# A written-out list of steps, one PSUM pool, and unsplit band scores in every batch

## The chip, the core and the metric

The kernel runs on one core of one Trainium2 chip. The metric is the device time of one execution in microseconds (us). A profile shows the core's engines: PE is TensorE (PEld its weight loads), DVE is VectorE, ACT is ScalarE, POOL is GpSimd, SP issues the transfers.

## What is computed

Two layers follow each other, for 4 batches of 768 positions. Layer one is attention with 8 heads of 64 channels in which position i sees the 128 positions up to itself and the first 4 (the sinks). Its output x (768 x 512) goes into layer two: four experts, each a causal attention over all 768 positions with one head of 64 channels, weighted by a gate that keeps the best 2 of 4 experts.

```
scores = q @ k.T / 8 ;  keep = (key < 4) | (0 <= row - key < 128)        # layer one
x = softmax(where(keep, scores, -1e9)) @ v                               # per head, then heads side by side
logits = x @ w_gate ; w = softmax over the two largest                   # layer two
out = sum over the two experts e of  w_e * (causal_softmax((x wq_e)(x wk_e).T / 8) @ (x wv_e) @ wo_e)
```

Everything is float32. A matmul of the kernel either takes float32 operands as they are ("exact" in the code), or each operand is split into a rounded part and its remainder, both float32r, and three products are added up (`THREE`).

## The kernel before

The work is cut into units. A unit of kind 0 ("first") is a pair of heads of one batch in layer one: 16 of them. A unit of kind 1 ("second") is a pair of experts of one batch in layer two: 8 of them. Two heads (or experts) always go together: one lies on partitions 0 to 63, the other on 64 to 127.

A first unit loads q, k and v (`first`), turns q and k so that channels lie on partitions (`Pair.turn_by_pe` in batch 0 on PE, `Pair.turn` in the others on DVE, L799 and L803), computes scores row by row (128 positions each): `band_scores`, on PE, 260 columns (two key blocks and the sinks) or 128 in the first row. In batches 0 and 1 (`EXACT`) the scores are float32 matmuls of `qn` with `kx` (L820). In batches 2 and 3 ACT writes the rounded part (L804), POOL the remainder (L808), into the tiles `qs` and `ks`, and PE does three float32r matmuls per head (L825). Then DVE picks and takes the row minimum (L1078, L1081; L1047 in the first two rows), ACT takes exp (L1085, L1052), DVE sums (L866, L867), POOL scales (L1059, L1104), PE transposes the probabilities (L878), ACT or DVE copies them out of PSUM (L707, L709) or DVE multiplies them by a triangle (L922), and PE multiplies them with v into an accumulator `Acc` (L851, L855). The sum leaves PSUM as a rounded part and a remainder of x (L690 on ACT, L695 on DVE).

A second unit projects x (L1177, 48 matmuls for q and as many for k), splits the result into `qs` and `ks` (L757 on ACT, L760 on DVE), and does wide causal rows the same way (L825, L981, L989, L996, L878, L851). Per batch there are also the values and the gate (L1204) and the output projection (L1251).

PE's array is used in four ways: transposes ("ROWS" in the code) and scores ("rows") address it as two halves of 64 rows, 64*128 in a profile; L851 addresses it as two halves of 64 columns, 128*64 ("cols"); projections use all of it, 128*128 ("FULL"). L525 (`fill`) is a matmul of zeros that the planner puts where it sees PE idle within the first 130 us, L1262 ten such at the start.

What stands when on an engine is decided before the program is built. Every piece of work is a `Step` with a priority, a cost, the steps it comes after and the buffers that it makes and uses; `Plan.emit` simulates the five engines and always takes the step that can begin earliest, for PE by priority with a charge for changing the way the array is used. `NUDGE` adds to the priorities, by kind, unit and number. Buffers are rings, `kinds`: 6 PSUM banks for all but the accumulators (`b`), 2 for the accumulators (`acc`), 2 of each of `qs` and `ks`, 9 of `p` (probabilities), 3 of `pt` (transposed ones). A step can't be placed until its ring has a free slot.

Of the kernel before, what the change touches and what calls it, by code (L numbers as in the profile page):

```python
# [34 lines left out]
PSUM = ("b", "acc")  # L35

NUDGE = {
    "busy_PE": 5.2, " ": -68.2, " busy_PE": 82.2, " busy_PE 0": 78.2, "sink_values_DVE": 13.5, " sink_values_DVE": -16.5,
    "load_SP": -45.6, " load_SP": 39.9, "again_SP": 20.9, " again_SP": 56.7, "sink_values_ACT": -27.6,
    " sink_values_ACT": 7.3, "sink_values_POOL": 52.1, " sink_values_POOL": 35.8, "sink_values_SP": -45.0,  # L40
    " sink_values_SP": -24.6, "weight_ACT": -52.5, " weight_ACT": 53.4, "weight_POOL": -34.8, " weight_POOL": 46.3,
    "000 ": -73.5, "000 load_SP": -144.1, "tr_PE": -1.9, "000 tr_PE": -132.5, "000 tr_PE 0": -105.3, "fn_DVEACT": -11.6,
    "000 fn_DVEACT": 132.8, "000 tr_PE 1": -54.6, "go_POOL": 0.7, "000 go_POOL": -36.7, "000 tr_PE 2": -47.6,
    "000 tr_PE 3": -19.2, "spread_POOL": -14.3, "000 spread_POOL": -25.7, "differences_POOL": 6.4,
    "000 differences_POOL": 24.4, "band_scores_PE": 0.5, "000 band_scores_PE": -115.3, "000 band_scores_PE 0": 8.1,
    "low_DVE": -53.0, "000 low_DVE": -79.5, "exp_ACT": 45.8, "000 exp_ACT": 63.9, "go_DVE": -42.9, "000 go_DVE": -204.0,
    "norm_POOL": -27.0, "000 norm_POOL": -84.7, "000 tr_PE 4": 23.5, "av_PE": -0.2, "000 av_PE": -0.9, "000 av_PE 0": -50.3,
    "000 band_scores_PE 1": -19.2, "000 tr_PE 5": -41.0, "000 av_PE 1": -26.4, "000 band_scores_PE 2": -53.5,
    "pick_DVE": -45.8, "000 pick_DVE": -22.7, "000 band_scores_PE 3": -19.7, "keep_POOL": -10.3, "000 keep_POOL": 6.5,
    "000 tr_PE 6": 35.3, "tri_DVE": -62.4, "000 tri_DVE": 59.9, "of_sinks_PE": -0.3, "000 of_sinks_PE": -1.5,  # L50
# [241 lines left out]
}  # L292

HURRY = 30.10
STAY = 41.79
BULK = -8.35
FILL_COST, FILL_KEEP, FILL_END = 220.0, 0.0, 130000.0
# [26 lines left out]
class Step:  # L324


    def __init__(self, prio, cost, fn, after, new, use, moves, mode, behind):
# [15 lines left out]
        for b in (*new, *use):  # L343
            b.users.append(self)


class Plan:
# [31 lines left out]
    def emit(self):  # L379
# [19 lines left out]
        for s in self.steps:  # L399
            if not s.waiting:  # L400
                put(s)
# [955 lines left out]
```

## Time and profile before

| | |
|---|---|
| median of 3 runs | 393.12 us (392.98 to 393.4) |
| span of the profiled execution, first to last instruction | 391.6 us |
| the execution's own time | only its span is recorded; the runs' median is 1.5 us above it |
| PE, DVE, ACT, POOL busy | 383.9, 309.4, 271.7, 261.1 us |
| matmul records on PE | 4508 |

Busy time is the union of an engine's records. Matmuls are pipelined and the ends of their records are modelled, so one that waits for its turn inside the array still counts as busy; what a group of matmuls costs is better read from the starts of the records. A float32 matmul has two records, a float32r one has one.

### The profile page before, as it was taken

The numbers are of one execution on the slowest core, as the hardware profiler recorded it, in microseconds if no ns is written. First come the engines' busy times: TensorE is split into PE (matmuls) and PEld (weight loads), VectorE is DVE, ScalarE is ACT, GpSimd is POOL, SyncE is SP. The second block draws the span as 40 slices with busy tenths as digits, with TensorE's granted clock in tenths as the row PEclk, the third lists the DMA queues.
The fourth block names the chain that finished last, engine by engine and source line by source line (L and its number), as shares of the span: only waits on it lengthen the run. The fifth ranks groups of instructions, "written<-read, shape, count | busy, mean of one in ns | idle before, by whom it ended". The sixth has DMA issues, their size and how long they took to land.

```text
span 391.6 us, 12873 instructions
## 1 busy us (share of the span) xinstructions
PE 383.9 (98%) x4508; PEld 325.8 (83%) x4508; DVE 309.4 (79%) x1424; ACT 271.7 (69%) x971; POOL 261.1 (67%) x461
## 2 busy tenths in 40 slices
PE   8999999999999999999999999999999999999995
PEld 7767878988888888988888888988888888987874
DVE  6899998787999969679889959688689806648943
ACT  3898986266999957468869958459678804717830
POOL 5669999236999983568959854479958730038840
PEclk9999999999999999999999999999999999999999
DMA  7989997321165251523506100223000000012003
GB/s 164 224 159 169 186 181 131 56 42 44 42 109 97 44 107 56 83 83 83 82 3 121 44 0 5 40 110 95 2 3 2 3 3 2 2 54 110 3 28 134
DMA packets 124032, 28.42 MB, mean 73 GB/s; under 512 B 120576, under 2 KB 120576, under 8 KB 123968
## 3 DMA queue, kind: packets, MB, share of 16 engines
q1 hardware_dynamic: 123968, 27.61, 33.7%
q8 instruction: 35, 0.57, 0.6%
q14 instruction: 29, 0.24, 0.2%
HBM read 21.05 MB, written 6.29 MB: 70 GB/s over the span
## 4 chain that ended last, share of the span: by engine, by line
PE 83%; DVE 8%; POOL 3%; issue 2%; ACT 2%; DMA 1%; POOLq 0%; ACTq 0%; SPq 0%; DVEq 0%
PE acc L851 18%; PE b L1177 18%; PE b L825 13%; PE b L878 11%; PE b L1204 9%; PE b L1251 9%; PE b L820 4%; DVE b L1078 1%; DVE p L1081 1%; PE b L1262 1%; PE acc L855 1%; POOL p L1059 1%; DVE p L981 1%; DMA vn<-in_v_dram 1%; POOL v L680 1%
## 5 line engine op out<-in xcount | busy, mean ns | idle before, releaser
L996 POOL TENSOR_TENSOR p<-p,st 128x128 f32<-128x128 f32 (+5 forms) x96 | 87.3, 935 | 1.3
L707 ACT ACTIVATE pt<-b 128x256 f32<-128x256 f32 (+3 forms) x175 | 63.4, 397 | 12.5 <-PE b L878 8.8
L989 ACT ACTIVATE p<-p,st 128x384 f32<-128x384 f32 (+5 forms) x96 | 63.6, 669 | 9.4 <-DVE st L981 9.0
L825 PE MATMUL b<-ks,qs 64*128 64x260 f32 (+4 forms) x672 | 69.4, 323 | 0.3 <-DVE pt L922 0.2
L825 PEld LDWEIGHTS b<-ks,qs 64*128 64x128 f32 x672 | 52.9, 186 | 4.7 <-ACT pt L707 0.9
L878 PE MATMUL b<-ident,p 64*128 64x64 f32 x1120 | 55.1, 228 | 0.2 <-POOL p L1059 0.2
L878 PEld LDWEIGHTS b<-ident,p 64*128 64x128 f32 x1120 | 44.3, 138 | 11.7 <-issue 6.4
L1085 ACT ACTIVATE p<-p,st 128x132 f32<-128x132 f32 x128 | 51.1, 407 | 3.8 <-DVE st L1081 3.6
L981 DVE CUSTOM_DVE_ANT_0 p<-b,cmask 128x384 f32<-128x384 f32 (+3 forms) x96 | 45.3, 506 | 1.4 <-PE b L825 1.1
L851 PE MATMUL acc<-pt,v 128*64 128x128 f32 x672 | 45.5, 278 | 0.6 <-DVE pt L709 0.5
L851 PEld LDWEIGHTS acc<-pt,v 128*64 128x64 f32 x672 | 36.2, 136 | 7.1 <-issue 3.9
L851 PE MATMUL acc<-pt,vn 128*64 128x128 f32 x448 | 41.5, 283 | 0.3 <-ACT p L989 0.3
L709 DVE COPY pt<-b 128x256 f32<-128x256 f32 (+3 forms) x81 | 34.6, 446 | 8.3 <-PE b L878 7.9
L1204 PE MATMUL b<-wvh,x 128*128 128x260 f32 x192 | 35.8, 285 | 0.0
L1059 POOL TENSOR_TENSOR p<-p,st 128x520 f32<-128x520 f32 (+1 forms) x32 | 26.5, 835 | 13.5 <-DVE st L867 9.8
L1177 PE MATMUL b<-x,wqh 128*128 128x256 f32 (+1 forms) x128 | 33.2, 344 | 0.1
L1104 POOL TENSOR_TENSOR p<-p,st 128x512 f32<-128x512 f32 x32 | 33.2, 1041 | 0.0
L1177 PE MATMUL b<-x,wkh 128*128 128x512 f32 (+1 forms) x128 | 32.8, 341 | 0.0
L1251 PE MATMUL b<-woh,y 128*128 128x512 f32 x96 | 32.7, 402 | 0.0
L1081 DVE CUSTOM_DVE_ANT_0 p<-b,pair_mask 128x132 f32<-128x132 f32 x128 | 32.6, 288 | 0.0
L1078 DVE COPY_PREDICATED b<-earlier,b 128x128 f32<-128x128 int32 x128 | 31.2, 287 | 0.5 <-PE b L820 0.3
L1052 ACT ACTIVATE p<-p,st 128x260 f32<-128x260 f32 (+1 forms) x64 | 29.0, 459 | 3.7 <-DVE st L1047 2.9
(132 smaller groups left out, 919.0 us busy)
## 6 DMA issues: line engine op xcount, KB each, us to landing
vn<-in_v_dram SPq DMA_DIRECT2D x32, 192.0 KB, 3.2
out_dram<-o SPq DMA_DIRECT2D x24, 256.0 KB, 2.0
qn<-in_q_dram SPq DMA_DIRECT2D x52, 96.0 KB, 2.4
kn<-in_k_dram SPq DMA_DIRECT2D x52, 96.0 KB, 2.4
qn<-in_q_dram SPq DMA_DIRECT2D x6, 192.0 KB, 4.2
kn<-in_k_dram SPq DMA_DIRECT2D x6, 192.0 KB, 4.3
o<-in_moe_wo_dram SPq DMA_DIRECT2D x2, 256.0 KB, 3.7
v<-in_moe_wk_dram SPq DMA_DIRECT2D x4, 128.0 KB, 3.5
```

The source lines that it names most:

```text
L707: nc.scalar.activation(dst(), src(), AF.Copy)
L825: nc.tensor.matmul(o, self.qs.t[hs, a, qs], self.ks.t[hs, b, ks], start=n == 0, stop=n == 2)
L851: nc.tensor.matmul(o[e * 64:e * 64 + 64], lhs, rhs, start=e not in self.begun, stop=last and self.done == len(self.steps))
L878: nc.tensor.transpose(t[g].t[:, n, :], x[gs], ident[gs, gs])
L981: nc.vector.tensor_tensor_reduce(out=one(e)[:, cs], in0=s2[e].t[:, :(c1 - c0) * 128], in1=mask(c0, c1), scale=times, scalar=st.t[:, 3, es] ...
L989: nc.scalar.activation(x, x, AF.Exp, bias=st.t[:, 0, es], scale=-1.0, accum_out=st.t[:, 1, es])
L996: nc.gpsimd.tensor_mul(x, x, st.t[:, 2, e:e + 1].to_broadcast([128, n * 128]))
L1081: nc.vector.tensor_tensor_reduce(out=p.t[:, n, :], in0=s2[e].t[:, :SW], in1=pair_mask, scale=-scale, scalar=BIG, op0=OP.add, op1=OP.min, a ...
L1085: nc.scalar.activation(p.t[:, n, :], p.t[:, n, :], AF.Exp, bias=st.t[:, 0, n:n + 1], scale=-1.0, accum_out=st.t[:, 1, n:n + 1])
L1177: nc.tensor.matmul(t.t, w[a][:, c, es], X[b, c].t[:, x, cs], start=c == 0 and m == 0, stop=c == NCH - 1 and m == 2)
L1204: nc.tensor.matmul(t.t[:, :VW], X[b, c].t[:, a, qs], W["wv"][w][:, c, :], start=c == 0 and n == 0, stop=c == NCH - 1 and n == 2)
L1251: nc.tensor.matmul(t.t, Y[b, c].t[:, a, qs], W["wo"][w][:, c, :], start=c == 0 and n == 0, stop=c == EP - 1 and n == 2)
```

## The change

- `NUDGE`, `HURRY`, `STAY`, `BULK` and the search in `emit` go. A string `ORDER` lists all 2702 steps by number; a letter behind a number says which engine does a copy that ACT and DVE could both do (281 `a`, 119 `v`). `emit` goes through the list, gives each step its buffers, and issues it. What an engine does follows the list. `lined_up` stands for other shapes only.
- `fill_in` is the old fill rule, on the times that the list gives.
- `EXACT` is (0, 1, 2, 3): the split of q and k in layer one (ACT L804, POOL L808) and its three products per head are gone in batches 2 and 3; there too scores are float32 matmuls of `qn` with `kx`.
- `qs` and `ks` have one buffer each, used by second units only. `p` has 11, `pt` has 4. The accumulators share one pool of 8 PSUM banks with all else.

In both programs PE does the same transposes (1280), the same L851 (688), sinks (64) and projections (816). Float32 score matmuls go from 96 to 192, float32r ones from 672 to 384, fills from 44 to 10.

```diff
-PSUM = ("b", "acc")
-NUDGE = {
-    "busy_PE": 5.2, " ": -68.2, " busy_PE": 82.2, " busy_PE 0": 78.2, "sink_values_DVE": 13.5, " sink_values_DVE": -16.5,
...
-HURRY = 30.10
-STAY = 41.79
-BULK = -8.35
+PSUM = ("b",)
+ORDER = """
+0 46 1 52 44 49 53a 54v 51v 50a 64 65 39 55 40 75 78 41 47 45 76 59 60a 86 90 61a 67 56 58v 57v 93 79 143 87 91 77 80 81 142
...
     def emit(self):
-        for s in self.steps:
-            s.prio += sum(NUDGE.get(name, 0.0) for name in s.part)
...
+        listed = ORDER.split()
+        if len(listed) == len(self.steps):
+            order = []
+            for word in listed:
+                s = self.steps[int(word.rstrip("av"))]
+                order.append((s, {"a": ACT, "v": DVE}.get(word[-1]) or next(iter(s.cost))))
+        else:
+            order = self.lined_up()
+        free, moved, mode = dict(FREE), 0.0, "FULL"
+        for s, e in order:
+            t, taken = max([0.0] + [p.end + LATENCY[p.eng, e] for p in s.after] + [p.begun for p in s.behind]
+                           + [b.idle(e) for b in s.banks]), {}
+            for b in s.new:
+                at, n = self.slot(b.tag, e, taken.get(b.tag, ()))
+                taken.setdefault(b.tag, []).append(n)
+                b.slot, t = n, max(t, at)
...
             if e == PE and free[PE] < FILL_END:
...
+                self.fill_in(free[PE], t + turn, mode, s.mode)
...
+            s.fn()
...
-    kinds = {"qn": (3, 768, F32), "kn": (2, 768, F32), "vn": (3, 768, F32), "qs": (2, 2 * S, F32R), "ks": (2, 2 * NB * SW, F32R),
+    kinds = {"qn": (3, 768, F32), "kn": (2, 768, F32), "vn": (3, 768, F32), "qs": (1, 2 * S, F32R), "ks": (1, 2 * NB * SW, F32R),
-             ... "p": (9, 768, F32), "dv": (2, 512, F32), "pt": (3, 1024, F32), ...
+             ... "p": (11, 768, F32), "dv": (2, 512, F32), "pt": (4, 1024, F32), ...
-             "b": (6, 512, F32), "acc": (2, 512, F32)}
+             "b": (8, 512, F32)}
...
-            self.b = buf("acc", 512)
+            self.b = buf("b", 512)
...
-    EXACT = (0, 1)
+    EXACT = (0, 1, 2, 3)
```

What the list does to the order is seen on the engines. First PE, in the last batch's second units, behind their last scores. Before (L825 scores, L851 probabilities times values into an accumulator, L878 transposes):

```order
L825 MATMUL b_122<-ks_73,qs_72 128x384
L851 MATMUL acc_126<-pt_98,v_0_83 64x128 x6
L878 MATMUL b_124<-ident,p_87 128x64
L878 MATMUL b_123<-ident,p_87 128x64
...
L851 MATMUL acc_126<-pt_99,v_0_83 64x128 x6
L878 MATMUL b_121<-ident,p_88 128x64
L878 MATMUL b_120<-ident,p_88 128x64
...
```

and now, at the same place (L652, L678 and L705 are the same three; `b_127` is the accumulator):

```order
L652 MATMUL b_120<-ks_72,qs_71 128x384
L705 MATMUL b_121<-ident,p_93 128x64
L705 MATMUL b_125<-ident,p_93 128x64
...
L678 MATMUL b_127<-pt_98,v_0_81 64x128 x6
L678 MATMUL b_127<-pt_97,v_0_81 64x128 x6
L678 MATMUL b_127<-pt_100,v_0_81 64x128 x4
L705 MATMUL b_124<-ident,p_90 128x64
```

Before, four transposes stand between two pieces of column work and the array turns to columns for six matmuls at a time; now sixteen matmuls on three `pt` buffers follow each other. Over the program the column stretches (L851 and fills, 128*64) number 92 before and 56 now. Split at the first projection: 21 and 71 before, 12 and 44 now. The turns between FULL and the 64-row ways go from 29 to 41 behind the first projection. Between the last score of one second unit and the first of the next (seven such places) PE's row now has 104 to 254 other matmuls; the fewest, 104, are 36 of a projection with 512 columns, 44 transposes, 20 L851 and 4 band scores.

Second DVE, just ahead of the write of x that the first projection waits for (L695, the fourth tile x of batch 0). Before (L1078 pick, L1081 and L1047 row minimum, L799 turning of k):

```order
L799 STREAM_TRANSPOSE kx_82<-kn_67 128x3x128
L922 TENSOR_TENSOR pt_99<-b_120,own 128x4x64
L922 TENSOR_TENSOR pt_99<-b_124,own 128x4x64
L1081 ISA p_87,st_116<-b_123,pair_mask 128x132
...
L1047 ISA p_86,st_113<-b_121,bmask_138 128x128
L1047 ISA st_113 128x1
L695 SCALAR_TENSOR_TENSOR x_78<-acc_125,x_78 128x512
```

and now (L905, L908, L749, L626, L522 are the same statements):

```order
L749 TENSOR_TENSOR pt_98<-b_126,own 128x4x64
L905 COPY_PREDICATED b_124<-earlier,b_124 128x128
L908 ISA p_88,st_115<-b_124,pair_mask 128x132
L908 ISA st_115 128x1
L626 STREAM_TRANSPOSE kx_80<-kn_67 128x3x128
L522 SCALAR_TENSOR_TENSOR x_76<-b_121,x_76 128x512
L874 ISA p_94,st_117<-b_123,bmask_139 128x128
```

The row minimum of the next unit's first row (now L874) has moved behind the write. Counted from the program's start up to and with that write, DVE does 207 pieces of work before and 202 now: four copies of turned q or k fewer (they went to ACT), two copies of `pt` fewer and four of `sk` more, three first-row minima fewer, two turnings on DVE fewer, one pick and one minimum more.

## Rows read from the trace of the kernel before

**Rows 1.** The page, parts 1 and 2: busy time of PE and DVE, granted clock

```profile
PE 383.9 (98%) x4508; PEld 325.8 (83%) x4508; DVE 309.4 (79%) x1424; ACT 271.7 (69%) x971; POOL 261.1 (67%) x461
...
PEclk9999999999999999999999999999999999999999
```

**Rows 2.** Windows: us, busy PE, PEld, DVE, ACT, POOL, PEclk, DMA share, GB/s

```profile
10.00:20.00 10.00, 9.73 (x132) 7.25 (x129) 8.96 (x55) 8.76 (x41) 7.10 (x15) 1.00 1.02 224
...
120.00:140.00 20.00, 19.92 (x271) 17.36 (x269) 19.71 (x91) 19.59 (x70) 19.18 (x32) 1.00 0.35 67
```

**Rows 3.** Timeline at the first projection: start, us, engine, line, tiles, count

```profile
53.31 0.69 DVE L695 SCALAR_TENSOR_TENSOR x<-acc,x 128x512 fp32r<-128x512 f32 x1
...
53.93 0.74 PE L1177 MATMUL b<-x,wqh 128*128 128x512 f32 x2
```

**Rows 4.** Groups of DVE from 0 to 54 us: busy us, mean ns, idle before

```profile
L1081 DVE CUSTOM_DVE_ANT_0 p<-b,pair_mask 128x132 f32<-128x132 f32 x36 | 9.3, 285 | 0.0
L1078 DVE COPY_PREDICATED b<-earlier,b 128x128 f32<-128x128 int32 x37 | 9.2, 285 | 0.5 <-PE b L820 0.3
...
L1047 DVE CUSTOM_DVE_ANT_0 p<-b,bmask 128x128 f32<-128x128 f32 x11 | 2.8, 282 | 0.1
...
L709 DVE COPY kx<-b 128x192 f32<-128x192 f32 x7 | 2.3, 351 | 1.2 <-PE b L878 1.2
L799 DVE STREAM_TRANSPOSE qn<-qn 128x384 f32<-128x384 f32 x4 | 2.2, 560 | 0.0
```

**Rows 5.** Timeline of PE where the array turns, at 121 and at 234 us

```profile
121.38 0.41 PE L878 MATMUL b<-ident,p 64*128 64x64 f32 x8
121.61 1.27 PE L825 MATMUL b<-ks,qs 64*128 64x384 f32 x12
122.81 0.88 PE L851 MATMUL acc<-pt,vn 128*64 128x128 f32 x12
123.62 0.28 PE L878 MATMUL b<-ident,psk 64*128 64x64 f32 x2
123.73 0.41 PE L878 MATMUL b<-ident,p 64*128 64x64 f32 x8
124.07 0.44 PE L851 MATMUL acc<-pt,vn 128*64 128x128 f32 x4
...
234.32 1.77 PE L851 MATMUL acc<-pt,v 128*64 128x128 f32 x28
236.02 1.09 PE L878 MATMUL b<-ident,p 64*128 64x64 f32 x28
```

**Rows 6.** Timeline of PE: three band-score steps in a row, exact, then split

```profile
110.56 1.57 PE L820 MATMUL b<-kx,qn 64*128 64x260 f32 x12
112.06 0.88 PE L851 MATMUL acc<-pt,v 128*64 128x128 f32 x12
...
182.64 1.76 PE L825 MATMUL b<-ks,qs 64*128 64x260 f32 x18
184.34 0.88 PE L851 MATMUL acc<-pt,v 128*64 128x128 f32 x12
...
202.54 1.31 PE L825 MATMUL b<-ks,qs 64*128 64x260 f32 x18
203.78 0.66 PE L851 MATMUL acc<-pt,vn 128*64 128x128 f32 x8
```

**Rows 7.** Groups by line, whole span: the remainder of q, wide splits, fills

```profile
L808 POOL TENSOR_TENSOR qs<-qn,qs 128x384 fp32r<-128x384 f32 x16 | 16.3, 1017 | 3.4 <-ACT qs L804 3.2 <-DMA vn<-in_v_dram 0.2
...
L760 DVE TENSOR_TENSOR qs<-b,qs 128x512 fp32r<-128x512 f32 (+1 forms) x16 | 8.8, 553 | 15.3 <-ACT qs L757 15.3
...
L757 ACT ACTIVATE qs<-b 128x512 fp32r<-128x512 f32 (+1 forms) x16 | 7.9, 492 | 13.6 <-PE b L1177 13.4
...
L525 PE MATMUL b<-nought 128*64 128x128 f32 x60 | 4.5, 286 | 0.0
```

**Rows 8.** The chain that ended last, merged: start, us, engine, line, count

```profile
310.02 17.15 PE b L1177 x96
```

More of the change, by code (lines that the diff above doesn't have):

```diff
@@ L300 @@
+FREE = {PE: 2000.0, DVE: 4500.0, ACT: 4000.0, POOL: 5300.0, SP: 650.0}
+FILL_COST, FILL_END = 220.0, 130000.0
 class Buf:
@@ L329, in __init__ @@
         self.after, self.waiting, self.then, self.begun = [], 0, [], None
-        self.end, self.eng, self.part = None, None, ""
+        self.end, self.eng = None, None
         for b in new:
@@ L342, in __init__ @@
         self.banks = [b for b in use if b.tag in PSUM]
-        for b in (*new, *use):
+        self.of = list(dict.fromkeys((*new, *use)))
+        for b in self.of:
             b.users.append(self)
@@ L352, in __init__ @@
         self.steps = []
-        self.part, self.made = "", {}
         self.held = {tag: [None] * n for tag, n in rings.items()}
@@ L361, in step @@
         self.steps.append(s)
-        names = fn.__qualname__.split(".")
-        kind = (names[-3] if "<lambda>" in names[-1] else names[-1]) + "_" + "".join(cost)
-        number = self.made[self.part, kind] = self.made.get((self.part, kind), -1) + 1
-        s.part = (kind, f"{self.part} ", f"{self.part} {kind}", f"{self.part} {kind} {number}")
         return s
@@ L377, in slot, with lined_up @@
         return best
-    def emit(self):
-        for s in self.steps:
-            s.prio += sum(NUDGE.get(name, 0.0) for name in s.part)
+    def lined_up(self):
         for line in self.fifo.values():
@@ L389, in emit @@
                     b.waiting += 1
-        free = {PE: 2000.0, DVE: 4500.0, ACT: 4000.0, POOL: 5300.0, SP: 650.0}
-        ready = {e: [] for e in ENGINES}
-        def put(s):
-            s.at = {e: max([0.0] + [p.end + LATENCY[p.eng, e] for p in s.after] + [p.begun for p in s.behind])
-                    for e in s.cost}
-            for e in s.cost:
-                ready[e].append(s)
-        for s in self.steps:
-            if not s.waiting:
-                put(s)
-        order = []
@@ L403, in emit @@
-        left = len(self.steps)
-        moved, mode = 0.0, "FULL"
-        while left:
-            best = None
-            for e, steps in ready.items():
-                cand = None
-                bulk = {"full": 0.0, "rows": 0.0, "cols": 0.0}
-                if e == PE:
-                    for s in steps:
-                        if s.at[PE] <= free[PE] + 300.0:
-                            bulk[s.mode.lower()] += s.cost[PE]
-                for s in steps:
-                    t, taken = max([s.at[e]] + [b.idle(e) for b in s.banks]), {}
-                    for b in s.new:
-                        at, n = self.slot(b.tag, e, taken.get(b.tag, ()))
-                        if at is None:
-                            t = None
-                            break
-                        taken.setdefault(b.tag, []).append(n)
-                        t = max(t, at)
-                    if t is None:
-                        continue
-                    if e == PE:
-                        t += LATE.get((mode, s.mode), 0) - SWITCH.get((mode, s.mode), 0)
-                    t = max(t, free[e])
-                    key = (s.prio + (STAY - BULK * min(bulk[s.mode.lower()], 2500.0) / 1000.0 if s.mode.lower() != mode.lower() else 0.0) + HURRY * (t - free[e]) / 100.0, t) if e == PE else (t, s.prio)
-                    if cand is None or key < cand[0]:
-                        cand = (key, s, t)
-                if cand is not None and (best is None or cand[2] < best[1]):
-                    best = (cand[1], cand[2], e)
-            assert best is not None, "no step can go on"
-            s, t, e = best
-            if e == PE and free[PE] < FILL_END:
-                where = [(tag, n) for tag in PSUM for n in range(len(self.held[tag]))
-                         if (self.held[tag][n] is None or (self.held[tag][n].free_at(PE) or 1e9) <= free[PE])]
-                kept = "FULL" if mode == "FULL" else "cols"
-                spare = (t + SWITCH.get((mode, s.mode), 0) - free[PE] - SWITCH.get((mode, kept), 0) - SWITCH.get((kept, s.mode), 0) - FILL_KEEP)
-                if spare > FILL_COST and where:
-                    f = Step(0.0, {}, lambda x=(kept, where[0], int(spare / FILL_COST)): self.fill(*x), (), (), (), 0, kept, ())
-                    f.eng, f.begun = PE, free[PE]
-                    f.end = free[PE] + SWITCH.get((mode, kept), 0) + int(spare / FILL_COST) * FILL_COST
-                    order.append((free[PE], len(order), f))
-            s.eng, s.begun, s.end = e, t, t + s.cost[e]
@@ new lines, in lined_up @@
+        left = {b: len(b.users) for s in self.steps for b in s.new}
+        held = {tag: [None] * len(slots) for tag, slots in self.held.items()}
+        ready, order = [s for s in self.steps if not s.waiting], []
+        while ready:
+            for s in sorted(ready, key=lambda s: s.prio):
+                at = {tag: [n for n, b in enumerate(held[tag]) if b is None or not left[b]] for tag in held}
+                if all(len(at[tag]) >= sum(b.tag == tag for b in s.new) for tag in {b.tag for b in s.new}):
+                    break
+            else:
+                raise AssertionError("no step can go on")
+            ready.remove(s)
+            order.append((s, next(iter(s.cost))))
+            for b in s.new:
+                held[b.tag][at[b.tag].pop(0)] = b
+            for b in s.of:
+                left[b] -= 1
+            for n in s.then:
+                n.waiting -= 1
+                if not n.waiting:
+                    ready.append(n)
@@ new lines, in lined_up, with emit @@
+        return order
+    def emit(self):
+        listed = ORDER.split()
[4 more added lines that the diff above has]
+                order.append((s, {"a": ACT, "v": DVE}.get(word[-1]) or next(iter(s.cost))))
+        else:
+            order = self.lined_up()
[3 more added lines that the diff above has]
+                           + [b.idle(e) for b in s.banks]), {}
+            for b in s.new:
+                at, n = self.slot(b.tag, e, taken.get(b.tag, ()))
+                taken.setdefault(b.tag, []).append(n)
+                b.slot, t = n, max(t, at)
+            turn = SWITCH.get((mode, s.mode), 0) if e == PE else 0
+            if e == PE:
+                t += LATE.get((mode, s.mode), 0) - turn
+            t = max(t, free[e])
+            if e == PE and free[PE] < FILL_END:
+                self.fill_in(free[PE], t + turn, mode, s.mode)
+            s.eng, s.begun, s.end = e, t, t + turn + s.cost[e]
@@ L446, in emit @@
             if e == PE:
-                s.end += SWITCH.get((mode, s.mode), 0)
                 mode = s.mode
@@ L452, in emit, with fill_in @@
                 s.end = moved + 1000
-            for x in s.cost:
-                ready[x].remove(s)
-            taken = {}
-            for b in s.new:
-                b.slot = self.slot(b.tag, e, taken.get(b.tag, ()))[1]
-                taken.setdefault(b.tag, []).append(b.slot)
             for b in s.new:
                 self.held[b.tag][b.slot] = b
+                b.t = b.make()
             for b in s.banks:
                 b.read[e] = s.end
-            order.append((t, len(order), s))
-            for n in s.then:
-                n.waiting -= 1
-                if not n.waiting:
-                    put(n)
-            left -= 1
-        self.length = max(free.values())
-        for _, _, s in order:
-            for b in s.new:
-                b.t = b.make()
-            s.fn()
+            s.fn()
+    def fill_in(self, since, until, mode, then):
+        where = [(tag, n) for tag in PSUM for n in range(len(self.held[tag]))
+                 if (self.held[tag][n] is None or (self.held[tag][n].free_at(PE) or 1e9) <= since)]
+        kept = "FULL" if mode == "FULL" else "cols"
+        spare = until - since - SWITCH.get((mode, kept), 0) - SWITCH.get((kept, then), 0)
+        if spare > FILL_COST and where:
+            self.fill(kept, where[0], int(spare / FILL_COST))
 @with_exitstack
@@ L1311 @@
         b, n, kind = u
-        plan.part = f"{b}{n}{kind}"
         if kind == 0:
```

124 lines of the change are left out of this document (105 added, 19 removed), and 238 rows, old and new, of the table NUDGE.

## The prediction

> **What bounds the kernel now.** I read the busy times first: PE is busy 98% of the span, the next engine, DVE, 79% [rows 1]. So the sum of what PE does is nearly the time, and the two questions are how many of PE's nanoseconds the change takes away and where PE is not the one that sets the pace. The clock is no question before: the granted clock is full, 2.4 GHz, in every slice [rows 1].
>
> The windows answer the second question. From 10 us on DVE is busy 9.0 of 10 us and ACT 8.8 [rows 2], though the page calls PE busy there too: part of that is fills and waits inside the array. The first projection starts at 53.93 us, just after DVE began, at 53.31 us, the write of x on which it waits [rows 3]. Up to that point DVE, which has to pick, reduce and copy for four first units, sets the pace; PE's work there has room. Behind it, PE runs to the end with few gaps in its records [rows 1], and with one more stretch, at 120 to 140 us, where DVE (19.71 of 20 us), ACT and POOL are full as well [rows 2].
>
> So I count the start by DVE and the rest, 391.6 - 53.9 = 337.7 us, by PE.
>
> **The start.** Up to and with the write of x, DVE's row has 207 pieces of work before and 202 now. Fewer: four copies of turned q or k at 0.351 us, three first-row minima at 0.282, two turnings at 0.560; more: one pick and one minimum, 0.285 each [rows 4]. That is -1.40 - 0.85 - 1.12 + 0.57 = -2.8 us. The two `pt` copies fewer and the four short `sk` copies more I let cancel; between nothing and 0.35 us each they are worth -0.7 to +1.4. Neighbours on DVE overlap a little: 36 minima of 0.285 us would be 10.3 us and took 9.3 [rows 4], so I take nine tenths: **-2.5 us**, between -3.2 and -1.0. Of the 44 fills 34 go and of the 21 column stretches before that point 9 go; as PE has room there, I count them at nothing. Their cover is DVE's pace; if that pace were no bound, they would be worth the price given under the rivals.
>
> **Fewer turns of the array, behind the first projection.** What a turn costs is read from starts. Out of the column way: twelve L851 records start 0.81 us before the next transposes, twenty-eight 1.70 us before them [rows 5]. Sixteen records more cost 0.89, so twelve cost 0.67, and 0.14 is left for turning out. Into it: eight transposes behind a `psk` pair start 0.23 us ahead of scores (same 64-row way) and 0.34 us ahead of L851 [rows 5]: 0.11 for turning in. Column stretches go from 71 to 44 in this part: 27 x (0.14 + 0.11) = **-6.8 us**. I hold this firm to a quarter, -5.1 to -8.5. Turns between FULL and the 64-row ways go from 29 to 41. No row here has one by itself; bounded by nothing and by the dearer column turn, 12 x 0 to 12 x 0.14, and nearest to the cheaper turn: 12 x 0.11 = **+1.3 us**.
>
> **Band scores, exact for split, in batches 2 and 3.** Forty steps of 260 columns change (eight units, five rows). Three exact ones in a row start 1.50 us ahead of the column work that follows; three split ones 1.24 us in one place and 1.70 in another [rows 6]. Both runs end with the same turn, so the change per step lies between (1.50 - 1.70)/3 = -0.07 and (1.50 - 1.24)/3 = +0.09 us, -2.8 to +3.6 us in all. The 1.24 us run is the one without waits in it, but the exact run may hold one too; I take +0.05: **+2.0 us**. The eight steps of 128 columns I put at nothing, with the same 0.09 us each as their bound, 0.7 us to either side.
>
> The Trainium skill (FP8 and Floating Point Precision, "TensorE Precision Notes") says that true float32 takes four passes through the array; the split takes three of one pass. By that rule a step pays one pass of 260 columns more, which at 2.4 GHz is an estimated 0.11 us, or +4.3 us for the forty, and the whole sum would come out 2.3 us later. The trace puts the difference lower [rows 6], as the split has six weight loads where the exact step has two matmuls; by the measured rows it is +2.0.
>
> **Waits inside the score runs.** The 0.46 us between the two split runs is time in which PE stood though its records count as busy [rows 6]. The 240 records of such steps make thirteen runs of eighteen; at half of 0.46 us each, about 3 us are lost there. The change takes away one of the things that such steps wait for (POOL's 32 remainders at 1.0 us each [rows 7], and the ACT pass ahead of each) and the separate pool of banks. I take **-2.5 us**, from 0 to -5.
>
> **Edits at no cost of their own.** One buffer of `qs` and `ks`: hidden while PE has other work between second units; its price is the second rival. Eleven `p`, four `pt`, one pool: they only take waits away, which are counted above. Copies moved between ACT and DVE: both have room behind the start, and are priced ahead of it. Fills behind the start: there are none in either program. The transfers: the same loads and stores are issued on SP, whose queue is the bound only for the first load; I count them at nothing.
>
> **The sum.** -2.5 - 6.8 + 1.3 + 2.0 - 2.5 = -8.5 us on the profiled 391.6 us: 383.1 us. The median of the runs lies 1.5 us above the span, so 384.6 us.
>
> **Rivals.**
>
> DVE sets the pace for longer. For it: at 120 to 140 us all three side engines are full [rows 2], and the list hands more picks and minima to DVE ahead of the same PE work. Then the start gains nothing and PE's savings up to 140 us, 86 of 338 us or a quarter of -6.0, come to nothing: -4.5 us, 388.6 us. Against it: DVE's total falls (20 copies fewer), and PE has projections from 54 us on to stand between.
>
> PE waits at each change of second unit (slower). With one `qs` and one `ks` the next unit's split can't begin before the last score of this one. The price is four ACT passes of 0.49 us and the last DVE pass of 0.55 us, [rows 7], 2.5 us in which no score can start; seven such places make 17.6 us, 402.2 us. It decides where PE's row has less than 2.5 us of other work between those scores. Against it: the fewest there are 104 matmuls, 36 of them projections, and projections take 17.15 / 96 = 0.18 us each [rows 8], so 6 us at the least. It would need these projections to be the ones that wait: they fill PSUM banks that the late split has to empty, and four of eight banks are then held.
>
> The start is bound by PE after all. Then the fills count: 88 records, 60 of which took 4.5 us [rows 7], so nearer 55 ns each by the slope of L851 [rows 5], 4.8 us, and nine column stretches at 0.25, 2.3 us: the start gives 7.1 instead of 2.5 us. With the upper end of the waits, -5 us, that makes 377.5 us. For it: a DVE idle by a tenth at 10 to 20 us [rows 2]. Against it: the projection that starts right at DVE's write [rows 3].
>
> The clock falls. With 34 fills fewer PE may stand still more in the first 50 us. At 1.2 GHz for 10 us of them PE's 9.7 us of work there [rows 2] would take twice as long: up to +9.7, 394.3 us. Against it: the clock is full in all slices [rows 1], and the list leaves only ten places with a fill because it sees PE at work in the others. The Trainium skill (TensorE: Matmul & The Clock Gate, Part 1) has the clock halved by default and full only while PE is kept busy; the trace before never shows the halved level, so no row here bears it out.
>
> That the change does nothing is ruled out by the rows of its order, where stretches are joined and the remainders of q and k are gone.
>
> **How the numbers follow.** The forecast, 384.6 us, gets 0.50, and by its own bounds 379 to 390. DVE's pace 0.14, PE at the start 0.20, the change of units 0.06, the clock 0.04; 0.06 for several small losses that end near or above the time before. What a measurement can tell from no change is about 0.2%, 0.8 us. Faster than 392.3 us are the forecast, the first and the third rival, and a little of the rest: 0.86; within 0.8 us: 0.05; slower: 0.09. The range, 376.5 to 391.5 us, leaves out the slower cases and the far end of the fast one.
>
> **What would show it.** Right: the first projection near 51.5 us with DVE full ahead of it; column stretches followed by transposes at 0.14 us as before, but fewer; three exact steps in 1.5 us in batches 2 and 3; POOL about 30 us less busy, and PE's busy share still 98%. Wrong: PE gaps in front of L652 wide scores released by `qs` or `ks`; a granted clock below 1.00; the first projection at 54 us or later; exact steps at 0.6 us each.

## The result, and the profile after

The changed kernel takes 379.2 us (median of 4 runs, 378.32 to 379.82), the kernel before 393.08 us on the same chip: a ratio of 0.9644, 95% interval 0.963 to 0.9658. The forecast was 384.6 us with a range of 376.5 to 391.5 us: the side and the range hold, and the gain was 13.9 us instead of 8.5.

The profiled execution has a span of 376.6 us, 15.0 us less than before. It is the fastest of its four runs, 0.9 us under their median, so 0.9 of the 15.0 us are luck of that run. First the page (parts 1 and 2, as in [rows 1]):

```profile
span 376.6 us, 12371 instructions
...
PE 367.9 (98%) x4344; PEld 319.2 (85%) x4344; DVE 303.4 (81%) x1404; ACT 270.2 (72%) x959; POOL 230.8 (61%) x429
...
PEclk9989999999999999999999999999999999999999
```

PE is the engine that is full, as before. POOL has lost the remainders of q and k, 30 us. New is the 8 in the row of the granted clock. The windows of [rows 2], with the stretch between them:

```profile
10.00:20.00 10.00, 8.13 (x91) 6.04 (x87) 9.70 (x65) 9.75 (x45) 9.02 (x18) 1.00 0.89 199
20.00:30.00 10.00, 9.39 (x113) 7.71 (x114) 8.46 (x53) 9.12 (x43) 9.17 (x15) 0.83 1.04 180
...
120.00:140.00 20.00, 20.00 (x221) 16.83 (x221) 16.08 (x71) 16.90 (x53) 11.42 (x16) 1.00 0.56 104
```

From 10 to 20 us PE is busy 8.13 us where it was 9.73; from 21.05 to 24.46 us its records show the granted clock at 0.5, which is 1.2 GHz. At 120 to 140 us DVE, ACT and POOL are no longer full. The first projection (as [rows 3]) starts at 50.99 us instead of 53.93, again behind DVE's write of x, and right behind other work of PE:

```profile
50.04 0.69 DVE L522 SCALAR_TENSOR_TENSOR x<-b,x 128x512 fp32r<-128x512 f32 x1
...
50.67 0.39 PE L678 MATMUL b<-pt,dv 128*64 128x128 f32 x4
...
50.99 0.73 PE L1004 MATMUL b<-x,wqh 128*128 128x512 f32 x2
```

The last record ahead of it starts 0.20 us before it, which is what PE takes at other turns from this form to the whole array too. So it was before, with 0.21 us; there the work ahead of the projection at 53.93 us was

```profile
53.48 0.53 PE L855 MATMUL acc<-sk,vs 64*128 64x128 f32 x2
```

I then added, over all PE records of both traces, the time from each start to the next start, and sorted these intervals by what the record does. An interval in which the array changes its form holds the record's own time and the turn. The record's own time is taken as the mean of the intervals of its shape that hold no turn, both traces together, and stands with its kind; the rest is the turn's, with whatever wait lies in it.

| us | before | after | difference | forecast |
|---|---|---|---|---|
| up to the first projection | 53.9 | 51.0 | -2.9 | -2.5 |
| behind it: turns between rows and columns (133, now 81) | 20.1 | 11.5 | -8.6 | -6.8 |
| turns from and to the whole array (38, now 48) | 4.6 | 6.1 | +1.5 | +1.3 |
| scores, banded and wide | 63.5 | 60.6 | -2.9 | +2.0 price, -2.5 waits |
| transposes, column and sink products | 107.3 | 104.8 | -2.5 | 0 |
| products over the whole array | 137.9 | 138.6 | +0.7 | 0 |
| from the start of the last product | 4.3 | 4.2 | -0.2 | 0 |

The sum is -15.0 us against -8.5 (the rows are rounded). Three terms are off by more than an us: column turns (1.8 us too small a gain), scores (-2.9 for -0.5), and transposes, column and sink products, which the forecast put at nothing. Why the start came out near its forecast is a further question, since the half clock was not in it.

### The profile page after: what moved, and what is told of

Its sections match the earlier page's. It is cut to its first block, busy times and chain, and to the rows that moved or that the text cites. A ratio compares the mean times of both kernels' runs of the same rounds, so it can differ in the third digit from the quotient of the medians.

```text
span 376.6 us, 12371 instructions
## 1 busy us (share of the span) xinstructions
PE 367.9 (98%) x4344; PEld 319.2 (85%) x4344; DVE 303.4 (81%) x1404; ACT 270.2 (72%) x959; POOL 230.8 (61%) x429
## 3 DMA queue, kind: packets, MB, share of 16 engines
HBM read 21.05 MB, written 6.29 MB: 73 GB/s over the span
## 4 chain that ended last, share of the span: by engine, by line
PE 81%; DVE 7%; POOL 5%; ACT 4%; issue 2%; POOLq 0%; ACTq 0%; DVEq 0%
PE b L678 19%; PE b L1004 16%; PE b L647 11%; PE b L705 10%; PE b L1031 9%; PE b L1078 8%; PE b L652 7%; POOL p L823 3%; ACT p L912 1%; PE b L682 1%; DVE p L808 1%; ACT p L816 1%; DVE b L905 1%; DVE p L874 1%; DVE p L908 1%
## 5 line engine op out<-in xcount | busy, mean ns | idle before, releaser
L816 ACT ACTIVATE p<-p,st 128x768 f32<-128x768 f32 (+5 forms) x96 | 63.6, 664 | 10.1 <-DVE st L808 9.6
L647 PE MATMUL b<-kx,qn 64*128 64x260 f32 (+1 forms) x384 | 53.8, 389 | 1.6 <-DVE qn L536 1.1
L705 PE MATMUL b<-ident,p 64*128 64x64 f32 x1120 | 54.7, 227 | 0.0
L705 PEld LDWEIGHTS b<-ident,p 64*128 64x128 f32 x1120 | 46.5, 139 | 9.4 <-issue 5.0
L808 DVE CUSTOM_DVE_ANT_0 p<-b,cmask 128x384 f32<-128x384 f32 (+3 forms) x96 | 46.2, 505 | 2.9 <-PE b L652 2.1
L678 PE MATMUL b<-pt,v 128*64 128x128 f32 x672 | 41.7, 275 | 0.2 <-ACT pt L534 0.2
L647 PEld LDWEIGHTS b<-kx,qn 64*128 64x128 f32 x384 | 35.3, 191 | 7.6 <-ACT qn L534 1.5
L652 PE MATMUL b<-ks,qs 64*128 64x384 f32 (+3 forms) x384 | 41.1, 337 | 0.0
L678 PE MATMUL b<-pt,vn 128*64 128x128 f32 x448 | 39.2, 280 | 0.0
L678 PEld LDWEIGHTS b<-pt,v 128*64 128x64 f32 x672 | 36.5, 137 | 3.0 <-issue 1.0
L697 POOL TENSOR_TENSOR st<-st,gate 128x2 f32<-128x2 f32 x48 | 9.3, 195 | 45.2 <-DVE st L694 27.4
L905 DVE COPY_PREDICATED b<-earlier,b 128x128 f32<-128x128 int32 x128 | 33.1, 287 | 3.7 <-PE b L647 3.3
L908 DVE CUSTOM_DVE_ANT_0 p<-b,pair_mask 128x132 f32<-128x132 f32 x128 | 34.4, 286 | 1.3
L1078 PE MATMUL b<-woh,y 128*128 128x512 f32 x96 | 35.1, 401 | 0.0
L1004 PE MATMUL b<-x,wqh 128*128 128x512 f32 (+1 forms) x128 | 33.3, 345 | 0.1
L1004 PE MATMUL b<-x,wkh 128*128 128x256 f32 (+1 forms) x128 | 33.1, 344 | 0.0
```

Source lines behind the costliest of these rows:

```text
L647: nc.tensor.matmul(o, self.q_of()[hs, qs], self.ks.t[hs, 0, ks], start=True, stop=True)
L652: nc.tensor.matmul(o, self.qs.t[hs, a, qs], self.ks.t[hs, b, ks], start=n == 0, stop=n == 2)
L678: nc.tensor.matmul(o[e * 64:e * 64 + 64], lhs, rhs, start=e not in self.begun, stop=last and self.done == len(self.steps))
L705: nc.tensor.transpose(t[g].t[:, n, :], x[gs], ident[gs, gs])
L808: nc.vector.tensor_tensor_reduce(out=one(e)[:, cs], in0=s2[e].t[:, :(c1 - c0) * 128], in1=mask(c0, c1), scale=times, scalar=st.t[:, 3, es] ...
L816: nc.scalar.activation(x, x, AF.Exp, bias=st.t[:, 0, es], scale=-1.0, accum_out=st.t[:, 1, es])
```

## Experiments

Every kernel was timed against the kernel before on the same chip, so ratios are compared: the changed kernel's is 0.9644. All edits are made to the changed kernel.

**The price of a band score.** In place of the float32 product, batches 2 and 3 do three float32r products, in the same order:

```
+ x = W["wv"][0].rearrange("p c n -> p (c n)")
+ for n in range(3):
+     for e, o in enumerate(outs):
+         hs = slice(e * 64, e * 64 + 64)
+         nc.tensor.matmul(o, x[hs, 260:388], x[hs, :ks.stop - ks.start], start=n == 0, stop=n == 2)
- nc.tensor.matmul(o, self.q_of()[hs, qs], self.ks.t[hs, 0, ks], start=True, stop=True)
```

> The changed kernel and its order of steps, but in batches 2 and 3 the banded scores are three float32r products again (their operands are a constant tile of the same shape, so those batches' scores are not the reference's; the float32 turns and every other step stay). The 40 steps of 260 columns and the 8 of 128 thus pay the price of before with nothing else changed. Theory A (the step cost 0.500 us split and 0.425 us unsplit in the two traces, and 4.14 against 2.58 us for the 128-column ones in all): 40 x 0.075 + 1.6 = +4.6 us over the changed kernel's 379.2, so about 383.8. Theory B (my prediction's price: unsplit 0.05 us dearer per 260-column step): 379.2 - 2.0 = 377.2. Theory C (PE is not the bound in those stretches): 379.2 within 0.5.

Measured: 377.99 us, ratio 0.9624 (0.9606 to 0.9642), 0.8 us less than the changed kernel with about 0.9 us to either side. Theory A is refuted, C fits within that error, and B's 2.0 us lie just outside it. The 0.500 and 0.425 us behind theory A were my misreading: such a mean holds the turn that follows the last score of a run, and the kernel before has more of these. The same three steps of batch 2 or 3, first in the changed kernel, then with three products (timeline of PE):

```profile
219.71 1.62 PE L647 MATMUL b<-kx,qn 64*128 64x260 f32 x12
221.26 1.97 PE L678 MATMUL b<-pt,v 128*64 128x128 f32 x32
```

```profile
219.50 1.57 PE L650 MATMUL b<-wvh 64*128 64x260 f32 x18
221.00 2.40 PE L686 MATMUL b<-pt,v 128*64 128x128 f32 x40
```

Where [rows 6] had 1.24 to 1.70 us, it is now 1.55 against 1.50 us from the first score to the column product: 0.017 us per step, 0.7 us for forty. All band scores behind the first projection, with the same turns behind them, sum to 28.96 us in the one trace and 28.90 us in the other.

**The price of a turn.** A small product is put at 62 places between column steps, once in row form and once in column form; in a third kernel the row form stands between steps that are in row form already:

```
+ if index in PROBES:
+     self.fill("probe_rows", PROBES[index], 1)
...
+ nc.tensor.matmul(to[:, :64], nought[g, :], nought[g, :64], start=True, stop=True)     # rows
+ nc.tensor.matmul(to[:64, :64], nought[:, :64], nought[:, :64], start=True, stop=True) # columns
```

> The changed kernel with 62 extra small products (64 x 128 stationary, 64 columns, float32, into a free bank that nobody reads), one between two column-tiled steps that follow each other on PE: each makes PE turn from columns to rows and back. To be set against the same 62 products in column form, which turn nothing. Theory A (a pair of turns costs 0.14 + 0.11 us, and PE is the bound throughout): 62 x 0.25 = 15.5 us longer than the column form. Theory B (part of a turn lies beside waits that are there anyway): less than 8 us longer.

> The control: the same 62 extra products at the same places in column form (128 x 64 stationary, 64 columns, float32), no turn added. Both theories: the products alone, an estimated 62 x 0.06 to 0.11 = 4 to 7 us over the changed kernel's 379.2, so 383 to 386.

Measured: 409.94 us in row form (ratio 1.0435, 1.0417 to 1.0452), 385.39 us in column form (0.981, 0.9792 to 0.9829). The difference is 24.6 us, 0.40 us per place: more than theory A's 0.25, and theory B is out. So the third kernel:

> The same 62 row-form products as in turns_rows, but each between two steps that are in row form already, so that no turn is added. It tells how much of the 24.6 us between turns_rows and turns_cols (0.40 us per place, where I had 0.25 for a pair of turns) is the row-form product's own. In the trace of turns_rows a place takes 0.203 us into the product, 0.160 between its two halves and 0.202 out of it; in turns_cols 0.166 in all. Theory A (the halves' 0.160 is the form's own, whatever stands around it, and a pair of turns is 0.30 or less): 62 x (0.16 + 0.04) = 12 us over the changed kernel, 391. Theory B (the whole 0.40 belongs to the turns, a row product alone is as cheap as a column product): 62 x 0.10 = 6 us, 385.

Measured: 389.55 us (ratio 0.9915, 0.9901 to 0.9928), 10.65 us over the changed kernel, where the column form costs 6.5. The form itself makes 4.15 us of the difference, between the two theories, and (24.55 - 4.15)/62 = 0.33 us are left for a pair of turns. The column kernel drops out of this sum; with the intervals of the other two ratios it is 0.31 to 0.35. This is rather an upper figure: between row steps a product lies beside its neighbours (in 39 of the 62 places their records stand between its two halves), so there it may cost less than it does alone. One place of turns_rows in the timeline of PE shows the two halves:

```profile
74.64 0.44 PE L688 MATMUL b<-pt,vn 128*64 128x128 f32 x4
75.01 0.43 PE L352 MATMUL b<-nought 64*128 64x64 f32 x2
75.37 0.66 PE L688 MATMUL b<-pt,vn 128*64 128x128 f32 x8
```

Four column records take 4 x 0.055 = 0.22 us by the slope of [rows 5]; the next start is 0.37 us later, so turning out costs 0.15 us. The row product takes 0.36 us with the turn back, and 10.65/62 = 0.17 us without one, so turning in costs 0.19. In the two kernels' own intervals, as in the table, turning out costs 0.15 us in both, turning in 0.15 before and 0.14 now, so a pair there is 0.28 to 0.30 us. The Trainium skill (TensorEngine Tiling (Array Packing), "Key Properties") says that a change of the tiling mode drains TensorE; these rows agree and give a price.

**The list left out.**

```
-ORDER = """ 0 46 1 52 ... 2700a 2701 """
+ORDER = ""
```

> The changed kernel without its list of steps: the order comes from the priorities alone (all scores unsplit, same pools). It turns 263 times between rows and columns where the list turns 104 times and the kernel before 175 times. Theory A (the order of steps carries most of the gain, at 0.12 us per turn and the waits that a poor order leaves): 159 more turns are +20 us over 379.2 before any wait, so over 399. Theory B (the unsplit scores and the pools carry the gain, the order matters little): at most 385.

Measured: 608.7 us, ratio 1.5499. Theory A has the side, and its 399 us are far too little: without the list PE waits as well (87% busy), and every copy that may go to ACT or DVE goes to DVE. From the groups by line of that kernel:

```profile
L601 PE MATMUL b<-ident,p 64*128 64x64 f32 x1120 | 74.8, 250 | 33.8 <-DVE pt L432 15.8 <-POOL p L719 13.5 <-DVE x L418 2.0
L248 PE MATMUL b<-nought 128*64 128x128 f32 x1168 | 69.4, 279 | 0.2 <-DVE st L804 0.2
```

Its mean granted clock is 0.903. It shows that unsplit scores and the pools don't make up for a poor order; it doesn't share the 229 us out between turns, waits, the clock and the 1168 filler records. Nor is it the order of the kernel before, which `NUDGE` and the search made: that order with these pools, or with unsplit scores, was not run, so how the 13.9 us are shared between the list and the pools is not shown.

**Does DVE pace the start?** My forecast counted the start by DVE's work.

```
- x = plan.step(at - LEAD_S, {DVE: 70 + 1.04 * 128}, pick, [mm], (), [s2[e]])
+ x = plan.step(at - LEAD_S, {DVE: 70 + 1.04 * 128}, pick if pair.batch else (lambda: None), [mm], (), [s2[e]])
```

> The changed kernel without the 32 predicated copies of batch 0 (the diagonal half of the two-row band scores of batch 0 is not picked, so those rows are not the reference's): 32 x 0.284 = 9.1 us less work on DVE before the first projection, the same order. Theory A (DVE paces the start, as my prediction had it): the first projection, at 50.99 us in the changed kernel, starts 4 to 9 us earlier, and the time falls as much, to 370 to 375. Theory B (PE bounds the start from 24 us on, where it is busy 3.9 to 4.0 of each 4 us): only PE's waits between 8 and 24 us can go, some 1.5 to 2.5 us: 376.7 to 377.7. Theory C (ACT or the pools hold it): 379.2 within 0.5.

Measured: 379.94 us, ratio 0.9671 (0.9658 to 0.9685): not faster. The windows of 10 to 30 us and, in the timeline, the first projection of this kernel:

```profile
10.00:20.00 10.00, 7.47 (x89) 5.90 (x89) 7.75 (x52) 9.66 (x44) 8.78 (x16) 1.00 0.82 186
20.00:30.00 10.00, 8.49 (x96) 6.76 (x97) 5.71 (x37) 8.37 (x40) 8.99 (x16) 0.83 0.95 170
```

```profile
52.16 0.73 PE L1005 MATMUL b<-x,wqh 128*128 128x512 f32 x2
```

DVE is 2 to 3 us emptier in each 10 us, PE stands still no less, and the projection comes no earlier. The half clock lasts 3.4 us in both profiles, so it doesn't hide a gain. DVE alone doesn't pace the start. In its place the chain of waits (start, us, what) had a load of q:

```profile
17.08 0.58 SPq L969
17.70 3.71 DMA qn<-in_q_dram
```

**Do the loads pace it?** Three kernels move the output weight's ten steps (34 to 43 of the list) from the first 26 us to behind the first projection, the second also the copies of the sink values (step 3) behind the next q load, the third also has no picks in batch 0:

```
-0 46 1 52 44 49 53a 54v 51v 50a 64 65 39 55 40 ...
+0 46 1 52 44 49 53a 54v 51v 50a 64 65 55 ... 39 40 41 42 43 34 35 36 37 38 607 ...
```

> The changed kernel with the ten steps of the output weight wo (two loads of 256 KB on SP's queue, four ACT copies, four POOL subtractions) moved in the list from the first 26 us to behind the first projection. It follows from the miss of no_picks_b0: without 9.1 us of DVE work the first projection did not come earlier, and the chain of waits there went over a q load issued at 17.08 us that landed at 21.4 us. Theory L (the loads pace the start: the two wo loads stand ahead of the q loads, 0.5 MB at the 230 GB/s of the first 20 us are 2.2 us): the first projection comes 1 to 2 us earlier, 377 to 378. Theory D (the chain through DVE and ACT paces it in the changed kernel, and the loads only once that is gone): 379.2 within 0.5. Theory P (PE's own work from 24 us on): the same within 0.5.

> As wo_later, and the three copies of the sink values (64 KB each, issued from 15.2 to 17.0 us) behind the q load that follows them. Theory L: another 0.6 to 1.7 us earlier for that q load, 376 to 377.5. Theories D and P: as wo_later, or later by up to 1 us where the sink products then wait.

> Both removals together: wo_later without the 32 predicated copies of batch 0 (so those rows are not the reference's). If DVE's chain and the loads each hold the start by themselves, taking either away shows nothing or little and taking both shows more than their sum: 374 to 376.5 (theories L and D together). If PE's work holds it (theory P): 379 within 1.

Measured: 380.83 us (ratio 0.969, 0.967 to 0.971), 380.96 (0.9684, 0.9663 to 0.9704) and 379.88 (0.9671, 0.9658 to 0.9684). No total falls, so theory L's totals are refuted. The first projection says more. It starts at 52.05 us in the first kernel and at 52.90 in the second, later than the changed kernel's 50.99, but their half clock lasts 6.8 us instead of 3.4. In the third the half clock lasts 3.4 us, as in the changed kernel and in the one without picks, and the projection starts here:

```profile
50.60 0.50 PE L1006 MATMUL b<-x,wqh 128*128 128x512 f32 x1
```

That is 1.6 us earlier than without picks alone (52.16) and 0.4 earlier than in the changed kernel, by one profile each. The total shows none of it, because in all three the part behind the first projection is 1.4 to 1.9 us longer (327.0 to 327.5 us; 325.6 in the changed kernel), where the moved steps now stand. So the loads and DVE together seem to hold the start by a little; DVE alone does not, and for the loads alone the longer half clock blurs the test.

**The clock.** Fewer fillers were the fourth rival's ground. One kernel has none, one has 40 products instead of 10 (its expectation says 20, which was a miscount), and the last one has the additional ones before 20 us only:

```
-FILL_COST, FILL_END = 220.0, 130000.0
+FILL_COST, FILL_END = 220.0, 0.0                                                  # none
+ if 8000.0 < since < 26000.0 and until - since > 60.0 and where:                  # more; 20000.0: early
+     self.fill(kept, where[0], max(2, int((until - since) / FILL_COST)))
```

> The changed kernel without its 10 filler products (20 records, 2.52 us of PE before 28 us). In the changed kernel the granted clock is at half from 21.05 to 24.46 us, after PE had idled 0.3 to 0.95 us in each 4 us from 4 to 24 us. Theory A (the fillers hold the clock up before 21 us): the half-clock stretch begins earlier and is longer, and the time grows by 1 to 3 us. Theory B (what ends the waits of the start is DVE, and PE has slack there): no change within 0.5 us, wherever the half clock falls.

> The changed kernel with 20 filler products instead of 10 (two or more at each expected wait of PE between 8 and 26 us at which a bank is free). Theory A (the half clock from 21.05 to 24.46 us costs time and comes from PE's idling): the stretch is gone, PE does the same work there in half the time, and up to 1.7 us are gained: 377.5. Theory B (PE has slack at the start, or the fillers stand in its way): 379.2 to 381, with or without the half clock.

> The changed kernel with the additional filler products of more_fills before 20 us only (24 products before 20 us instead of 8; after it the 2 of the changed kernel; more_fills had 40 in all, not the 20 that its expectation says). In more_fills the granted clock stayed at full throughout and yet the first projection came at 52.38 us: its fillers after 24 us, when PE no longer waits, stand for about 2 us there. Theory A (PE paces the start, and the half clock of 3 to 7 us costs it half of that): full clock throughout, the first projection at 50.0 to 50.5 us, and 0.5 to 1.5 us gained over the changed kernel: 377.7 to 378.7. Theory B (the start is held by loads, DVE or ACT): first projection at 51 to 52.4 as in all the others, 379.2 to 380.5.

Measured: none 379.11 us (ratio 0.9649, 0.9635 to 0.9662), more 381.0 us (0.9696, 0.9683 to 0.9709), early ones 378.05 us (0.9624, 0.961 to 0.9637). The windows of 16 to 28 us, without fillers, in the changed kernel, and with the early ones:

```profile
16.00:20.00 4.00, 2.62 (x29) 1.63 (x25) 3.90 (x29) 3.96 (x17) 3.92 (x8) 1.00 0.74 159
20.00:24.00 4.00, 3.81 (x35) 2.93 (x33) 3.05 (x19) 3.93 (x19) 3.56 (x7) 0.53 1.25 207
24.00:28.00 4.00, 4.00 (x38) 3.12 (x36) 3.38 (x22) 3.21 (x17) 3.92 (x9) 0.62 0.75 143
```

```profile
16.00:20.00 4.00, 3.05 (x29) 1.89 (x28) 3.90 (x26) 3.96 (x17) 3.65 (x9) 1.00 0.85 184
20.00:24.00 4.00, 3.39 (x35) 2.92 (x35) 2.60 (x16) 3.22 (x17) 3.84 (x5) 0.63 1.28 208
24.00:28.00 4.00, 4.00 (x50) 3.03 (x49) 3.90 (x25) 3.90 (x18) 3.92 (x10) 0.94 0.82 163
```

```profile
16.00:20.00 4.00, 3.36 (x49) 2.41 (x45) 3.90 (x27) 3.96 (x17) 3.83 (x7) 1.00 0.91 196
20.00:24.00 4.00, 3.50 (x47) 2.81 (x46) 3.62 (x23) 4.00 (x21) 3.65 (x6) 1.00 1.30 210
24.00:28.00 4.00, 4.00 (x53) 2.98 (x51) 3.93 (x25) 4.00 (x20) 3.92 (x10) 1.00 0.75 141
```

In these three the emptier PE is from 16 to 20 us, the longer the granted clock then stands at its lower level: from 20.24 us for 6.8 us without fillers, for 3.4 us in the changed kernel, not at all with the early ones. That order doesn't hold over all kernels here: without picks PE is busy 1.97 us there and the clock is down for 3.4 us, with the output weight later 3.12 us and 6.8 us. With the early fillers the first projection comes at 50.32 us, earlier than in any other kernel here:

```profile
50.32 0.50 PE L1006 MATMUL b<-x,wqh 128*128 128x512 f32 x1
```

With more fillers it is 52.38 us, at full clock all the same: those put behind 24 us, where PE has no wait left, are work in its way. So theory A holds for the early ones and B for the later ones. Taking all fillers out costs nothing beside the changed kernel: the 2.5 us that they take and the longer half clock seem to cancel. The kernel with the early ones beats both kernels by its median, 1.15 us under the changed one; the two ratios' intervals overlap a little (0.9637 and 0.963), so its lead is likely and not certain.

The runs of one kernel point the same way: the changed kernel took 378.32 us at a mean granted clock of 0.995, 379.10 at 0.993, 379.29 and 379.82 at 0.991; wo_sinks_later took 379.24 at 1.000, 379.83 at 0.994, 381.15 at 0.989, and 380.96 and 381.81 at 0.990. The five runs with early fillers lie at 0.998 to 1.000 and within 0.6 us. In the profiles a mean of 0.995 goes with 3.4 us at the lower level (changed kernel) and 0.991 with 6.8 us (no fillers), so the changed kernel's longer runs probably had the longer stretch, and the 0.9 us by which its profiled run was lucky are probably that.

## Why the prediction was right, and where its steps were not

- **Fewer column turns, -6.8 us.** Right in kind, too small: -8.6 us, just outside the -8.5 of its bound. Behind the first projection 52 fewer intervals hold a column turn, 26 pairs for the 27 that I counted. Turning out was read rightly (0.15 for 0.14); turning in a little low (0.14 to 0.15 in the kernels' own intervals, 0.19 by the inserted products, for 0.11): my base there was eight transposes ahead of scores, 0.23 us in [rows 5], and what of that was a wait no run measured. About 0.8 of the 8.6 us are waits that fell into such intervals: before, three of the 65 turns into columns lasted 0.34, 0.55 and 0.71 us where others behind the same product took 0.21, 0.20 and 0.15; now one does.
- **Waits, -2.5 us.** I expected them inside the score runs, and the size is about right: the scores' own time fell by 2.9 us, 1.3 of it in the steps of 260 columns, 0.9 in the wide ones, 0.7 in those of 128, and it is the same to 0.1 us with three products (60.5 us), so the form of the product didn't do it. What I left out is the 2.5 us at transposes, column and sink products; 0.9 of them are sixteen column records that moved ahead of the first projection. No experiment took one of these waits away by itself, so that what went is waits is argued, not shown.
- **Turns between whole array and rows, +1.3 us.** Measured +1.5 for ten more turns (twelve more with the rows, as I counted, and two fewer with the columns): 0.15 us each, where I had taken 0.11.
- **Exact for split scores, +2.0 us.** Too dear: exact costs 0.8 us more, within 0.9, and 0.7 by the starts shown. The 0.05 us per step came from the 1.24 us run of [rows 6]; 0.017 is what the same place shows at 1.55 and 1.50 us. By the rule of four passes (the Trainium skill, FP8 and Floating Point Precision, "TensorE Precision Notes") it would have been +4.3 us; the measurement decides against that price here. That the runs of [rows 6] "end with the same turn" was not right either: ahead of a turn into columns the last exact record of 260 columns takes 0.31 us from start to start in both traces, the last split one 0.20 to 0.21. That is 0.10 us more, near the 0.11 us estimated for one pass; what hides a further pass between the steps was not tried.
- **The start, -2.5 us.** The size (-2.9) was right by luck, and the step's reason failed: "DVE ... sets the pace; PE's work there has room". Without 9.1 us of DVE work nothing is gained. The projection right at DVE's write, on which I relied, was no sign of it. In both traces PE goes from other work straight into it, with no more time between than at other such turns (0.20 to 0.21 us). What did bring the projection earlier than in the changed kernel is PE's side, early fillers and the full clock (50.32 us), and, less, DVE's work and the loads taken away together (50.60). In the changed kernel it is the third and the fourth rival in one: PE has 4.1 us less of fillers (the rival's 4.8 us counted all 88 records, 20 of which stay) and nine column stretches fewer, waits 2.3 us more (gaps of over 50 ns between records 3.5 us, before 1.2) and loses some to the half clock. Which of DVE, ACT, loads and banks ends the 3.5 us that are left stays open: DVE's work brought nothing when it was taken away alone, the test of the loads alone is blurred by the half clock, and ACT and the banks were not tried.
- **The clock falls.** I gave it 0.04 and up to 9.7 us for 10 us of half clock. It happened, for 3.4 us, and so one of my signs of being wrong came true while the forecast held. What it takes can be gained back: 0.7 us at the first projection of the two profiles, 1.2 us by the medians. The trace before held only the full level; the fall at 21 us, behind 4 us in which PE was busy for 3.05, agrees with the rule of the Trainium skill (TensorE: Matmul & The Clock Gate, Part 1), clock down when PE is not kept busy.
- **One buffer of qs and ks.** Nothing to pay: no wait of PE for either stands among its waits in the trace after, and the scores' own time did not grow.

The net of it: -1.8 us in column turns, +0.2 in turns of the whole array, -2.4 in scores, -2.5 in transposes, column and sink products, +0.7 in products over the whole array, -0.4 and -0.2 at the two ends make, but for rounding, the 6.5 us by which the span fell further than forecast; less the 0.9 us of a lucky profile and 0.2 more around the span, it is the 5.4 us between 384.6 and 379.2. Nearly all of these errors lie on one side, gains that the forecast left out or priced too low.

## What to carry to other kernels

Where one engine is full, count how often its array changes form in the order of instructions, price a pair of changes by inserting one, and read the price of an operation only from intervals that hold no change. A full side engine in the windows doesn't show that it sets the pace: take work off it and see, and look at the granted clock and at the rest of the span before you believe the total. Fillers can pay ahead of the stretch where the clock would fall, and cost their time where PE no longer waits.

## What the runs showed of the hardware that was not expected

- A pair of turns rows to columns and back is 0.28 to 0.30 us in the kernels' own intervals and 0.33 by inserted products; ten more turns of the whole array went with 1.5 us.
- One float32 product and three float32r products of 260 columns on two 64-row tiles take the same time to 0.02 us in 0.5. Only ahead of a turn into columns does the last float32 record take 0.10 us longer than the last float32r one (0.31 and 0.21).
- The granted clock fell to half at 21.05 us in the changed kernel, with PE waiting in pieces of up to 0.88 us ahead of it, and came back at 24.46 us; without fillers it was down for about 7 us, with 26 of them not at all.
